# Clearing a slot table in eight paced parts, first gram matrices in one product, spare products from later on, and a new order of work

## The chip, the cores and the metric

The kernel runs on one core of one Trainium2 chip. The metric is the device time of one execution in microseconds (us), the median of several runs; lower is better. The core has a matrix engine (PE in the profile; its weight loads are shown as PEld), a vector engine (DVE), a scalar engine (ACT), a general engine (POOL) and a queue engine (SP) that issues most transfers. All of them run side by side and wait for each other by semaphores.

## The reference

Three stages follow each other. The attention is a delta rule over 768 steps for 2 x 8 heads of 48 columns; its output, 1536 rows of 384 columns, goes through a dense layer pair with a softmax-weighted hidden layer and a norm; the rows that come out are sent to one of 8 experts by the largest logit.

```python
for t in range(S):                                   # S = 768, per batch and head
    y[t] = q[t] @ state
    state = state + beta[t] * outer(k_n[t], v[t] - k_n[t] @ state)
h = x @ w_in                                         # 1536 x 384 by 384 x 1024
e = exp(h - max(h)); sm = e / sum(e)
solu = h * sm
ln = (solu - mean) / sqrt(var + 1e-6) * g_ln
x2 = ln @ w_out                                      # 1024 x 384
expert = argmax(x2 @ w_gate)                         # 8 experts, a capacity each
out = gate * (relu(slots @ w1[expert]) @ w2[expert]) # slots: rows of an expert in order of arrival
```

## The kernel before

The attention is done in 24 chunks of 32 steps, in three groups of eight chunks. For a group, gram matrices `G` (line 510) of k with k and of k with q are made on PE, masked on DVE or on ACT and POOL into `A` and `M`, `A` is transposed into `L` on DVE (586), the triangular system in `L` is solved there by some thirty small operations in two lines (595, 598), and transposed back into `Tt` and `Tn` (606, 608). Four pairs of products `Z` (628, 643) join the halves. Then the chunks go one after the other, since each needs the state that the one before it left: `X` (710) on PE, `R` (715) on DVE, two products (723), `ub` on ACT and DVE (731, 689), `dS` (738) on PE, the new state `S` on DVE (683), and `X` again (752). Four copies on ACT (673) take the chunk's output to `xt`; a chunk is then done, which the code calls the event `s1`. Norms of k (464 to 475) come ahead of a group.

The dense layers run beside that, a tile of 128 rows at a time: 18 products into `h` (905), a maximum, an exponential and a product on DVE and ACT (915, 919, 923), transposes `lp` (944), and 24 products into `xb` (954). Until the last chunk there is one buffer for `h`. Every finished tile's rows are scattered by an indirect transfer on POOL (1112) to their places in a table of slots, `xs`, in the chip's main memory. The table's rows must be cleared before that. After the last tile the experts follow (1389 and 1334 for most of them), from rows that are fetched from `xs`.

The order on PE, DVE, ACT and POOL is not the scheduler's: the build runs a planner (`Flow`), in which each chain of work is a generator that yields the engine it needs and a time, and waits for events; at each step the planner takes the chain of best rank, and the instructions are written out in that order. The ranks come from the table `PR`, so that one number moves work all over the first 340 us. Where the plan leaves PE idle long enough, `fill` writes a spare product (1241) that nobody reads. SP's queue takes its transfers in the order in which the planner came to them.

The clearing is the chain `clear` (line 430): one transfer of zeros from a tile `z` to the whole table (439), after which the event `clear` lets the chain `places` begin, which works out where the rows go.

Of the kernel before, what the change touches and what calls it, by code (L numbers as in the profile page):

```python
# [21 lines left out]
GC = 8  # L22
# [12 lines left out]
GATE, TOK, XW = DM, DM + 1, DM + 2  # L35
# [6 lines left out]
TURN = [b * TPB + s for s in range(TPB) for b in range(B)]  # L42
FIRST = [min(128, CAPS[0] - k) for k in range(0, CAPS[0], 128)]
LATE = 3
LAG = 1
WAIT = 0
LAG0 = 2
FILLER = 2
# [1 line left out]
EVA = (0, 1, 1)  # L50
HB = 0
HC = C // 2
PR = {'m0': 1.68, 'x0': 4.63, 'g1': 9.02, 'g2': 3.68, 'lg': 6.61, 'l1': 1.43, 'l2': 3.47, 'wi': 2.29, 'wo': 5.01, 'wog': 1.18, 'n1': 1.36, 'n2': 4.33, 'p1': 4.79, 'p2': 8.87, 'v': 8.16, 'y': 3.1, 'rows': 2.82, 'sx': 3.04, 'xt': 2.51, 'lt': 4.05, 'ft': 2.27}
PASSES = ((0, 0), (0, 1), (1, 0))
PE, DVE, ACT, POOL, DMA = range(5)
DENSE = 0
# [51 lines left out]
class Flow:  # L108
# [8 lines left out]
    def __init__(self, pace, cap, until):  # L117
        self.req = {e: [] for e in self.LAT}
        self.free = {e: 0.0 for e in self.LAT}
        self.pending = deque()  # L120
        self.cur = None
        self.rate, self.cap, self.fill = pace * self.COLS / self.TICK, cap, None
        self.level = self.at = 0.0
        self.floor, self.until = 1500, until if FILLER else 0
        self.cols = {}
        self.banks, self.fill_bank = {}, "h"
        self.mode, self.pool = DENSE, 0.0
        self.n = self.live = 0
# [69 lines left out]
    def run(self):  # L198
        while True:
# [3 lines left out]
            if not c:  # L203
                assert not self.live, "chains that wait for each other"
                return
            if self.fill:
                t = self.free[PE]
                n = min((x[0][0] for x in c if x[1] == PE), default=t + 9)
                if n - t < self.FILL[0] + (0.23 if self.warm(t) else 0.44):
                    t = n  # L210
                t = max(t, self._clear(self.fill_bank or "", PE))
                if any(self.fill_bank in r[5].split() and r[1] < t + 0.25 for o in self.req if o != PE
                       for r in self.req[o] if r[5] is not None):
                    t = n + 9
                if t < min(x[0][0] for x in c):
                    c = [((t, None), PE)]
# [63 lines left out]
def build(tc, I, out, cap, dbg=None, pace=1.15, room=100):  # L280
# [10 lines left out]
    with ctx:  # L291
# [24 lines left out]
        def us(nbytes):  # L316
            return nbytes / 220e3
# [113 lines left out]
        def clear():  # L431

            yield event("wo", FT - 1)
            yield DMA, us(NS * XW * 4)
            yield WT_
            z = wd.tile([128, XW], F32, name="z", tag="wT")
            nc.gpsimd.memset(z, 0.0)
            nc.gpsimd.memset(z[:, TOK:], FAR)
            nc.sync.dma_start(out=xs.rearrange("(n p) w -> p n w", p=128),
                              in_=z.unsqueeze(1).to_broadcast([128, NS // 128, XW]))  # L440
            WT_.release()
            event("clear").set()

# [109 lines left out]
        def prep(g):  # L555
# [9 lines left out]
                mw = one.tile([128, NI, C], F32, name="mw")  # L565
                fl.spawn(mask_w(g, mw), prio)
            AM[g] = (A, M, mw)
            if g:
                fl.spawn(grams(g, range(0, GC, 2), ((0, 1),)), PR['g1'] if g == 1 else PR['g2'])
            else:  # L570
                for k in range(2):
                    fl.spawn(grams(g, (0, 4), ((k,),)), prio + PR['m0'] * k)
                    fl.spawn(grams(g, (2, 6), ((k,),)), prio + PR['m0'] * k)
            if g:
                yield event("w", g)
            for c in range(0, GC, 2):
# [460 lines left out]
        def places():  # L1037
# [3 lines left out]
            for i, j in enumerate(TURN):  # L1041
                yield event("OH", j)
                pos, g, dist, ov = (posn[:, k, j:j + 1] for k in range(4))
                if i < NTILE - 1:
                    yield DVE, _dv(E)
                    nc.vector.tensor_tensor(out=CO[:, i + 1], in0=CO[:, i], in1=OH[:, j], op=ALU.add)
                    fl.loose()
# [512 lines left out]
```

## Time and profile before

| | us |
|---|---|
| median of 3 runs (495.34 to 499.2) | 498.14 |
| the profiled execution's own time | 496.29 |
| its span from the first to the last instruction | 494.4 |
| PE busy | 445.8 (90%) |
| DVE busy | 286.7 (58%) |
| ACT busy | 240.7 (49%) |
| POOL busy | 168.5 (34%) |

The span falls into four stretches: until 41.7 us the first group is prepared, until 292.8 us the chunks run with the dense layers beside them, until 343.8 us the rest of the dense layers, and then the experts. The profiled execution took 1.9 us more than its span. Its time lies within those of the three runs.

### The profile page before, as it was taken

Reading aid. Unit: us, or ns where it says so; the run is one execution under the profiler, and the core shown is the slowest. Engines: PE = TensorE matmul, PEld = TensorE weight load, DVE = VectorE, ACT = ScalarE, POOL = GpSimd, SP = SyncE. Lnnn points to the kernel's source line nnn. Section 1 sums busy time; section 2 is a strip of 40 time slices with the busy share of each in tenths; the row PEclk is TensorE's granted clock in tenths of the full one; section 3 lists DMA queues with packets and bytes.
Section 4 is the critical chain, followed back from the end, with each engine's and each line's share of the span. In section 5 each row is a group of like instructions: output and inputs, shape, how many; then the busy total and the mean of one; then the engine's idle time right before and its main releaser. Section 6 shows DMA issues by size and latency. Waiting matters only on the chain.

```text
span 494.4 us, 16769 instructions
## 1 busy us (share of the span) xinstructions
PE 445.8 (90%) x7220; PEld 380.1 (77%) x7220; DVE 286.7 (58%) x839; ACT 240.7 (49%) x556; POOL 168.5 (34%) x177
## 2 busy tenths in 40 slices
PE   7696697789949989799999999999999999999993
PEld 3446586667837777687777778898999999999993
DVE  5576486678713354787544466775465554654640
ACT  3012266756513333545445366762574775665620
POOL 1301454111200033211110023343486386669721
PEclk9696568959965989899999999999999999999998
DMA  8371335214390000000000014410887456586100
GB/s 300 84 306 57 103 116 184 66 38 177 125 339 8 3 21 21 3 16 18 20 3 3 4 38 141 153 57 19 294 320 249 158 188 211 189 293 210 75 24 27
DMA packets 16948, 57.58 MB, mean 116 GB/s; under 512 B 2328, under 2 KB 8326, under 8 KB 16098
## 3 DMA queue, kind: packets, MB, share of 16 engines
q1 hardware_dynamic: 15042, 51.70, 30.5%
q0 software_dynamic: 1824, 4.73, 2.6%
q8 instruction: 58, 0.95, 0.8%
q14 instruction: 24, 0.20, 0.1%
HBM read 45.96 MB, written 11.13 MB: 115 GB/s over the span
## 4 chain that ended last, share of the span: by engine, by line
PE 66%; DVE 9%; issue 9%; DMA 7%; ACT 5%; POOL 2%; SPq 1%; POOLq 0%; DVEq 0%; ACTq 0%
PE xb L954 11%; PE h L905 10%; PE u L1389 8%; PE o L1334 7%; PE X L710 5%; PE dS L738 4%; DMA out<-y,ti 3%; PE h L1241 3%; PE G L510 2%; PE X L752 2%; PE lp L944 2%; PE Z L643 2%; PE o L1427 2%; PE Z L628 1%; DMA xd<-xs 1%
## 5 line engine op out<-in xcount | busy, mean ns | idle before, releaser
L1206 POOL TENSOR_TENSOR wh<-wr,wh 128x512 fp32r<-128x512 f32 x64 | 81.7, 1304 | 24.6 <-ACT wh L1204 21.0
L905 PE MATMUL h<-wi,xT 128*128 128x512 f32 x216 | 66.0, 429 | 0.0
L954 PE MATMUL xb<-wo,lT 128*128 128x392 f32 x288 | 66.0, 369 | 0.0
L1334 PE MATMUL o<-wh,hT 128*128 128x384 f32 (+1 forms) x336 | 63.4, 341 | 0.3 <-DVE hT L1393 0.3
L1389 PE MATMUL u<-xdT,wh 128*128 128x240 f32 (+1 forms) x504 | 60.3, 278 | 1.0 <-DVE hT L1393 1.0
L1389 PEld LDWEIGHTS u<-xdT,wh 128*128 128x128 f32 x504 | 59.0, 189 | 1.6 <-DVE hT L1393 1.5
L1334 PEld LDWEIGHTS o<-wh,hT 128*128 128x128 f32 (+1 forms) x336 | 57.4, 182 | 0.8 <-DVE hT L1393 0.6
L954 PEld LDWEIGHTS xb<-wo,lT 128*128 128x128 f32 x288 | 52.4, 197 | 2.5 <-issue 0.5
L673 ACT COPY xt<-X 32x192 f32<-32x192 f32 x96 | 29.7, 310 | 37.4 <-PE X L752 36.2
L905 PEld LDWEIGHTS h<-wi,xT 128*128 128x128 f32 x216 | 39.8, 198 | 8.1 <-issue 0.7
L1204 ACT CAST wh<-wr 128x512 fp32r<-128x512 f32 x67 | 40.8, 616 | 5.8 <-DMA wr<-w 5.8
L1393 DVE SCALAR_TENSOR_TENSOR hT<-u,hT 128x240 fp32r<-128x240 f32 (+2 forms) x64 | 25.0, 409 | 28.8 <-ACT hT L1392 28.1
L710 PE MATMUL X<-S,kqT 48*64 48x48 f32 x768 | 32.2, 239 | 4.8 <-issue 2.8
L710 PEld LDWEIGHTS X<-S,kqT 48*64 48x64 f32 x768 | 28.7, 153 | 9.6 <-issue 5.2
L1392 ACT ACTIVATE hT<-u 128x240 fp32r<-128x240 f32 (+2 forms) x64 | 23.9, 376 | 22.3 <-PE u L1389 20.1
L731 ACT ACTIVATE ub<-X,slot 128x96 f32<-128x96 f32 x48 | 13.7, 335 | 34.6 <-PE X L723 34.2
L1346 POOL DMA_INDIRECT out<-y,ti x17 | 16.5, 972 | 37.6 <-ACT y L1322 11.0
L1112 POOL DMA_INDIRECT xs<-xo,posi x12 | 12.7, 1057 | 48.4 <-ACT lT L983 15.8
L715 DVE TENSOR_TENSOR R<-X,vt 128x384 f32<-128x384 f32 x24 | 13.3, 555 | 27.3 <-PE X L710 26.2
L738 PE MATMUL dS<-ub,kn 64*48 64x96 f32 x368 | 24.5, 284 | 3.5 <-ACT ub L731 3.4
L1241 PEld LDWEIGHTS <-ones 128*32 128x32 bf16 x168 | 13.6, 102 | 18.0 <-issue 6.3
L510 PE MATMUL G<-kqT 48*32 48x32 f32 (+1 forms) x1024 | 21.0, 233 | 6.9 <-issue 6.3
(197 smaller groups left out, 787.3 us busy)
## 6 DMA issues: line engine op xcount, KB each, us to landing
wr<-w SPq DMA_DIRECT2D x32, 768.0 KB, 5.1
kqT<-kqT SPq DMA_DIRECT2D x6, 1024.0 KB, 6.2
xs<-z SPq DMA_DIRECT2D x1, 5597.0 KB
w<-w_in SPq DMA_DIRECT2D x6, 512.0 KB, 4.1
w<-w_out SPq DMA_DIRECT2D x8, 384.0 KB, 3.2
kn<-kN SPq DMA_DIRECT2D x3, 768.0 KB, 8.5
vt<-vN SPq DMA_DIRECT2D x3, 768.0 KB, 11.2
xd<-xs SPq DMA_DIRECT2D x10, 193.0 KB, 4.9
```

Source lines behind the costliest of these rows:

```text
L510: nc.tensor.matmul(G[32 * r:32 * r + 32, c2 * 4 + Q], lhsT=kq[:, r1], rhs=x, start=True, stop=True)
L673: nc.scalar.copy(out=xt[s][32 * j:32 * j + 32, :, 96 * r:96 * r + 96] .rearrange("p b (l d) -> p b l d", l=2), in_=ps_[c % 2][p:p + 32, :, ...
L710: nc.tensor.matmul(ps[64 * o:64 * o + 64, q, r1], lhsT=T[p, c % HG, q // 2, r1, q % 2], rhs=S_[p, q, r1], start=(q == 0 and r1 == 0), stop ...
L738: nc.tensor.matmul(dS[64 * o:64 * o + D, q], lhsT=kn_t[g][64 * o:64 * o + 64, cc, q], rhs=ub[64 * o:64 * o + 64, q], start=False, stop=Tru ...
L905: nc.tensor.matmul(h[:, FH * n:FH * n + FH], lhsT=xT[a][:, k], rhs=wi[w][:, k, FH * n:FH * n + FH], start=(m == 0), stop=(m == 3 * KT - 1))
L954: nc.tensor.matmul(x2, lhsT=lT[t // 4][a][:, t % 4], rhs=wo[w][:, t], start=(t == 0 and i == 0), stop=(t == FT - 1 and i == 2))
L1204: nc.scalar.copy(out=hl[0][:, cs], in_=r[:, cs])
L1206: (nc.vector if k == 1 else nc.gpsimd).tensor_tensor(out=hl[1][:, cs], in0=r[:, cs], in1=hl[0][:, cs].bitcast(F32), op=ALU.subtract)
L1241: nc.tensor.matmul(spare[0], lhsT=ones[:, 0:32], rhs=ones[:, 0:spare[0].shape[1]], start=spare[0].shape[1] > 120, stop=True, skip_group_ch ...
L1334: nc.tensor.matmul(o, lhsT=hT[t][a][:, s:s + n], rhs=w[k][:, t % 4], start=(t == 0 and i == 0), stop=(t == FT - 1 and i == 2))
L1389: nc.tensor.matmul(u, lhsT=w[c][:, k, f0:f0 + 128], rhs=xT[a][:, k], start=(i == 0 and k == 0), stop=(i == 2 and k == KT - 1))
L1393: nc.vector.scalar_tensor_tensor(out=hh[1], in0=u, scalar=0.0, in1=hh[0].bitcast(F32), op0=ALU.max, op1=ALU.subtract)
```

## The change

The clearing is cut into eight transfers, of 3 or 4 times 128 rows of the table each. Each is preceded by a transfer of a single number from the output of chunk 9, 10, ... 16 to the first of the part's rows, so that the part is issued only once that chunk is done. The event `clear` comes after the fifth part, the new event `clear all` after the eighth; the third tile's placing waits for that one. The first group's gram matrices are made as those of the other groups are, k with k and k with q in one product of 64 columns, where there were two of 32. Spare products are written only from 28 us of the plan on; the limit that the planner was given before was not used. Several ranks in `PR` are new, and with them the order on every engine. `m0` was the rank step of the first group's grams, which is no longer read. No DVE, ACT or POOL instruction is added or removed.

```diff
-PR = {'m0': 1.68, 'x0': 4.63, 'g1': 9.02, 'g2': 3.68, 'lg': 6.61, 'l1': 1.43, 'l2': 3.47, 'wi': 2.29, 'wo': 5.01, 'wog': 1.18, 'n1': 1.36, 'n2': 4.33, 'p1': 4.79, 'p2': 8.87, 'v': 8.16, 'y': 3.1, 'rows': 2.82, 'sx': 3.04, 'xt': 2.51, 'lt': 4.05, 'ft': 2.27}
+PR = {'m0': 4.99, 'x0': 4.63, 'g1': 4.24, 'g2': 3.44, 'lg': 6.61, 'l1': 1.43, 'l2': 3.47, 'wi': 2.29, 'wo': 5.01, 'wog': 1.18, 'n1': 1.36, 'n2': 4.17, 'p1': 4.79, 'p2': 8.87, 'v': 8.16, 'y': 5.65, 'rows': 2.82, 'sx': 3.04, 'xt': 6.94, 'lt': 3.58, 'ft': 2.8}
...
-            if self.fill:
+            if self.fill and self.free[PE] >= self.until:
...
             yield event("wo", FT - 1)
-            yield DMA, us(NS * XW * 4)
             yield WT_
+            yield POOL, 0.5
             z = wd.tile([128, XW], F32, name="z", tag="wT")
             nc.gpsimd.memset(z, 0.0)
             nc.gpsimd.memset(z[:, TOK:], FAR)
-            nc.sync.dma_start(out=xs.rearrange("(n p) w -> p n w", p=128),
-                              in_=z.unsqueeze(1).to_broadcast([128, NS // 128, XW]))
+
+
+            n = NS // 128
+            at = [NCOL * i // CLEAR for i in range(CLEAR)] + [NCOL + (n - NCOL) * i // 3 for i in range(4)]
+            for i, (a, b) in enumerate(zip(at, at[1:])):
+                c = GC + 1 + i
+                yield event("s1", c)
+                yield from gate(xt[c // 4][32 * (c % 4):32 * (c % 4) + 1, 0, 0:1], xs[128 * a:128 * a + 1, 0:1])
+                yield DMA, us(128 * (b - a) * XW * 4)
+                nc.sync.dma_start(out=xs[128 * a:128 * b].rearrange("(n p) w -> p n w", p=128),
+                                  in_=z.unsqueeze(1).to_broadcast([128, b - a, XW]))
+                if b == NCOL:
+                    event("clear").set()
             WT_.release()
-            event("clear").set()
+            event("clear all").set()
...
-            if g:
-                fl.spawn(grams(g, range(0, GC, 2), ((0, 1),)), PR['g1'] if g == 1 else PR['g2'])
-            else:
-                for k in range(2):
-                    fl.spawn(grams(g, (0, 4), ((k,),)), prio + PR['m0'] * k)
-                    fl.spawn(grams(g, (2, 6), ((k,),)), prio + PR['m0'] * k)
+            fl.spawn(grams(g, range(0, GC, 2), ((0, 1),)), (prio, PR['g1'], PR['g2'])[g])
...
+                if i == 2:
+                    yield event("clear all")
```

SP's queue after the second group's weights and the third group's loads, before (`xs` is the table of slots, `z` the tile of zeros, `wr` the first expert's weights):

```order
L383 DMA kqT<-kqT 128x2048
L392 DMA vt<-vN 128x1536
L439 DMA xs<-z 128x29x386
L1183 DMA wr<-w 128x1536 x2
L1135 DMA x_4860<-xs 128x384
```

The same place after the change, up to the third part:

```order
L384 DMA kqT<-kqT 128x2048
L393 DMA vt<-vN 128x1536
L402 DMA xs<-xt 1x1
L449 DMA xs<-z 128x3x386
L402 DMA xs<-xt 1x1
L449 DMA xs<-z 128x3x386
L402 DMA xs<-xt 1x1
L449 DMA xs<-z 128x4x386
```

One transfer of 29 times 128 rows became eight pairs, and they stand between the last load of the attention and the first load of the experts, so nothing else in the queue waits behind them until the first expert's weights.

DVE in the last steps of the first group's solve, before (`sq` are squares of the second group's k, which its load must bring first; `nn` their sums):

```order
L598 TENSOR_TENSOR L<-L,tmp 128x2x4x11
L464 TENSOR_REDUCE nn<-sq 128x8
L595 TENSOR_TENSOR tmp<-L 128x72
L598 TENSOR_TENSOR L<-L,tmp 128x2x3x12
L595 TENSOR_TENSOR tmp<-L 128x52
L464 TENSOR_REDUCE nn<-sq 128x8
L598 TENSOR_TENSOR L<-L,tmp 128x2x2x13
L595 TENSOR_TENSOR tmp<-L 128x28
L598 TENSOR_TENSOR L<-L,tmp 128x2x14
L464 TENSOR_REDUCE nn<-sq 128x8
L600 MEMSET L 128x32
L606 STREAM_TRANSPOSE Tt<-L 128x32x32
```

The same stretch after:

```order
L605 TENSOR_TENSOR L<-L,tmp 128x2x4x11
L602 TENSOR_TENSOR tmp<-L 128x72
L605 TENSOR_TENSOR L<-L,tmp 128x2x3x12
L602 TENSOR_TENSOR tmp<-L 128x52
L605 TENSOR_TENSOR L<-L,tmp 128x2x2x13
L476 TENSOR_REDUCE nn<-sq 128x8
L602 TENSOR_TENSOR tmp<-L 128x28
L605 TENSOR_TENSOR L<-L,tmp 128x2x14
L607 MEMSET L 128x32
L476 TENSOR_REDUCE nn<-sq 128x8
L613 STREAM_TRANSPOSE Tt<-L 128x32x32
```

The first sum over the second group's squares stands four steps of the solve later, the second one six.

PE between the first product of chunk 8 and that of chunk 9, before (`xb` are the dense layers' products):

```order
L710 MATMUL X_136<-S,kqT 64x48 x16
L944 MATMUL lp<-idn,p 128x128 x4
L643 MATMUL Z<-z,Tn 32x16 x16
L723 MATMUL X_136<-R,Tt 32x48 x8
L723 MATMUL dS<-R,Tt 32x48 x8
L944 MATMUL lp<-idn,p 128x128 x4
L954 MATMUL xb<-wo_142,lT_2244 128x392
L954 MATMUL xb<-wo_143,lT_2244 128x392
L954 MATMUL xb<-wo_142,lT_2245 128x392
L954 MATMUL xb<-wo_142,lT_2244 128x392
L738 MATMUL dS<-ub,kn 48x96 x8
```

After:

```order
L717 MATMUL X_136<-S,kqT 64x48 x16
L840 MATMUL tp<-idn,wu 128x128 x3
L635 MATMUL Z<-Tt,A 32x16 x16
L730 MATMUL X_136<-R,Tt 32x48 x8
L730 MATMUL dS<-R,Tt 32x48 x8
L635 MATMUL Z<-Tt,A 32x16 x32
L745 MATMUL dS<-ub,kn 48x96 x8
L759 MATMUL X_136<-ub,M 32x48 x16
L635 MATMUL Z<-Tt,A 32x16 x16
```

The dense layers' products left the place, and small products of the second group's joins came to it. In counts over the whole order: ahead of chunk 8 there are 36 products into `h` where there were 54, and 18 into `xb` where there were 24; behind the first product of the last chunk there are 72 into `h` where there were 54, 138 into `xb` where there were 107, and 40 transposes `lp` where there were 32. Of spare products of 512 columns there is 1 where there were 90; of 120 columns into `xb` there are 75 where there were 13.

## Rows read from the trace of the kernel before

**Rows 1.** Page, part 2: busy tenths of PE and its clock in 40 slices.

```profile
PE   7696697789949989799999999999999999999993
PEclk9696568959965989899999999999999999999998
```

**Rows 2.** Stretches: length, then busy us (count) by engine, clock, DMA share, GB/s.

```profile
139.62:160.10 20.48, 17.02 (x260) 13.84 (x260) 5.80 (x16) 5.66 (x13) 1.31 (x3) 0.50 0.43 145
...
292.81:343.77 50.96, 49.53 (x421) 44.30 (x421) 33.16 (x138) 28.15 (x61) 17.39 (x21) 1.00 0.26 89
343.77:494.40 150.63, 141.35 (x1039) 138.99 (x1038) 76.88 (x174) 83.06 (x183) 90.04 (x75) 0.99 0.54 184
```

**Rows 3.** Timeline of the first group: start, length, engine, line, idle before.

```profile
13.35 0.76 DVE L528 TENSOR_TENSOR A<-G,mw 128x256 f32<-128x256 f32 x2 [2.02 <-POOL mw L551]
...
19.05 2.07 DVE L586 STREAM_TRANSPOSE L<-A 128x1024 f32<-128x1024 f32 x1
...
29.37 0.52 ACT L462 ACTIVATE sq<-kn 128x384 f32<-128x384 f32 x1 [4.69 <-DMA kn<-kN]
29.92 0.55 DVE L464 TENSOR_REDUCE nn<-sq 128x8 f32<-128x384 f32 x1 [2.31 <-ACT sq L462]
...
32.86 1.95 DVE L606 STREAM_TRANSPOSE Tt<-L 128x1024 f32<-128x1024 f32 x1
...
36.60 1.19 PEld L628 LDWEIGHTS Z<-Tt,A 32*32 32x32 f32 x128 [0.42 <-DVE M L528]
```

**Rows 4.** Chain that ended last, first 45 us: start, length, what.

```profile
18.30 1.93 PE G L510 x128
20.23 1.52 issue
...
38.51 1.95 issue
...
41.76 1.88 PE X L710 x32
```

**Rows 5.** Timeline around the clearing.

```profile
130.81 0.41 SPq L439 DMA_DIRECT2D xs<-z  x1
...
140.66 0.60 PE L643 MATMUL Z<-z,Tn 32*32 32x16 f32 x27 [4.29 <-issue]
...
147.82 1.01 PE L944 MATMUL lp<-idn,p 128*128 128x128 f32 x4 [2.42 <-issue]
```

**Rows 6.** Page, parts 3 and 6: instruction queue (packets, MB, share) and the clearing.

```profile
q8 instruction: 58, 0.95, 0.8%
...
xs<-z SPq DMA_DIRECT2D x1, 5597.0 KB
```

**Rows 7.** Chain that ended last, chunks 8 to 13.

```profile
162.37 1.06 PE X L710 x32
...
168.50 1.06 PE X L710 x32
...
177.38 1.33 issue
...
183.35 1.01 PE G L510 x32
```

**Rows 8.** Two us inside the clearing, and two beside the `G` at 183.35.

```profile
136.00:138.00 2.00, 0.37 (x7) 0.14 (x5) 0.56 (x1) 0.55 (x2) 0.30 (x1) 1.00 1.06 360
182.00:184.00 2.00, 2.00 (x78) 1.70 (x74) 1.20 (x5) 0.57 (x2) 1.97 (x4) 0.50 0.29 107
```

**Rows 9.** Chain that ended last, from the last chunk on.

```profile
292.81 1.13 PE X L710 x32
...
300.61 2.09 PE h L905 x9
...
303.46 4.31 PE xb L954 x24
...
331.70 1.10 PE x0p L1241 x19
```

More of the change, by code (lines that the diff above doesn't have):

```diff
@@ L44 @@
 LATE = 3
+CLEAR = 5
 LAG = 1
@@ L123, in __init__ @@
         self.level = self.at = 0.0
-        self.floor, self.until = 1500, until if FILLER else 0
+        self.floor, self.until = 1500, until
         self.cols = {}
```

## The prediction

> **What bounds the kernel now.** I read the slices of the page first, then the stretches, then the chain that ended last with the timeline beside it. The slices show PE busy at nine tenths or more in the last half, at full clock, and the holes in the first: slices where PE is at four to seven tenths, and its clock at five to nine [rows 1]. The experts take 150.63 us, 141.35 of it busy on PE, and the change leaves them alone; the rest of the dense layers ahead of them, behind the last chunk's first product, is 50.96 us with 49.53 busy [rows 2]. Both are bound by PE's own work. So what the change can win or lose lies ahead of 292.81, where that product starts [rows 9]: the time in which PE waits there, and the time in which it works at half clock. Two places concern the change.
>
> The first group is a chain with nothing beside it. The first masked write of `A` is at 13.35, the solve on DVE begins with the transposing at 19.05, and PE starts the first join at 36.60, after a late write of `M` [rows 3]. On the way DVE stands 2.31 us at a sum over the second group's squares, since the load of that k has landed only at 29.37 [rows 3].
>
> The clearing is one transfer of 5597 KB [rows 6], issued at 130.81 and moved at some 360 GB/s with the transfer engines full [rows 8]. PE stands 4.29 us until 140.66 and 2.42 us until 147.82 with no engine named that it waits for [rows 5], and works at half clock from 139.62 to 160.10 [rows 2]. Such stops have a pattern: between the one that ended at 18.30 and the next, 1.52 us long, PE ran exactly 128 loads and 128 products [rows 4], and the instruction queue moved 58 packets of 0.95 MB in all [rows 6], 16 KB each. I read the stops as PE waiting for its next piece of 256 instructions. Away from the clearing they take 1.3 to 2.0 us [rows 4, 7]; the longest stands inside it.
>
> **First group: 2.0 us less (0 to 3).** No spare product comes ahead of the grams now, so I price them at half clock, as at 183.35: 32 rows, which are 16 products of 64 columns, take 1.01 us [rows 7, 8], a pair of chunks 2.0. Two pairs can be done before the mask at 13.35. Each of the other two needs a buffer, free once `A` and `M` of an earlier pair are written, twice 0.4: the third runs from 14.2 to 16.2, the fourth to 18.3, and its `A` and `M` end at 19.1, where the transposing starts now at 19.05. The stop that ended at 18.30 goes with the smaller number of instructions, and half clock takes its place: no gain up to here. In the solve the first sum stands four steps later, and two sums stand ahead of the transposing instead of three. The load still lands at 29.4, the sum ends at 30.4, then two steps of 0.2, the second sum, and the transposing starts at 31.5 instead of 32.86. The join doesn't wait for `M` any more and starts at 33.5 instead of 36.60. Of these 3 us one is lost, since DVE has the remaining sums and a weight's splitting, some 3.5 us, ahead of the first joined write, and the stop of 1.95 us ahead of the second joins [rows 4] hangs on 256 instructions and stays. The first chunk's `X`, at 41.76 [rows 4], comes at 39.7.
>
> **Clearing: 6.4 us less (2 more to 14.2 less).** Now it costs 4.29 + 2.42 = 6.7 us of stops, and 17.02 us of PE's work at half clock [rows 2, 5]. `X` takes 1.88 us at half clock [rows 4] and 1.06 at full [rows 7], so 17.02 x (1 - 0.56) = 7.5 us would go at full clock; together 14.2. Two things come back. A part is 579 or 772 KB and fills the engines for 2.0 us at 360 GB/s, while chunks follow each other in 6.1 us (168.50 - 162.37) [rows 7]; so SP's queue keeps pace, and nothing stands behind a part in it. But each part may hold up a piece of instructions, by 0 to 2.0 us. PE takes a piece in some 4 us there, so about half the parts meet one, and I take half the bound: 8 x 0.5 x 1.0 = 4.0. And chunks 8 to 10 have the second group's joins beside them now, small products that use up pieces fast, in place of `xb`: a stop like the 1.33 us at 177.38 is to be expected, and shortly behind that one the clock stood at half as well [rows 7, 8]. So I let half of the 7.5 come back, 3.8. That leaves 14.2 - 4.0 - 3.8 = 6.4.
>
> The rows' placing starts later, after chunk 13, and for the third tile after chunk 16. Finished rows wait in six buffers, and the order has two placings ahead of chunk 17, so I cost this at nothing; if those buffers were full, `xb` would stop.
>
> [...]
>
> **New order: 1 us less (9 more to 5 less).** Ahead of chunk 8, PE has 18 products into `h` less, at 2.09 / 9 = 0.23 us, and 6 into `xb`, at 4.31 / 24 = 0.18 [rows 9]: 5.2 us that must be done later. Behind the last chunk's first product it has 18 and 31 more, 4.2 + 5.6, with the transposes some 11 us. PE's sum doesn't change, so this wins or loses only as far as the chunks come earlier by more or less than 11 us: the last chunk has to start at 282 to break even. I expect about that. The second group's solve stands beside chunks 4 to 6, where it stood beside 5 to 7, with its joins up to 141 as the last thing ahead of chunk 8 [rows 5]; but its steps stand close together on DVE there, and will hold up the chunks 4 to 6 themselves.
>
> **Spare products: 0.5 us more (0 to 3.6).** 62 more into `xb`, at 1.10 / 19 = 0.058 us [rows 9], are 3.6 us. They stand where the plan has PE idle, and cost only as far as the trace is later than the plan. The 89 large ones that go stood in waits for loads and for the solve, and give back nothing.
>
> **Sum.** 2.0 + 6.4 + 1.0 - 0.5 = 8.9 us less. On the profiled execution, 494.4 and 1.9 around it, that is 487.4; on the median of 498.14 it is 489.2. I take 488.3, midway.
>
> **Rivals.** *The clearing's cost is spread and not removed.* The same 5.6 MB go through the same engines, in the stretch where PE uses up pieces fastest. If nearly every part meets one, 8 x 2.0 = 16 us of stops stand against 14.2, the term is nothing, and 498.14 - 2.0 - 1.0 + 0.5 = 495.6 is left. For it: the 4.29 us stood in the middle of the clearing, not at its end. Against: gaps of 4 us between parts of 2 us leave a piece room. [...]
>
> *The chunks don't come earlier, and the dense work behind them does harm.* The place is behind chunk 23: 11 us more stand there. Chunks took 6.1 us each with PE's holes filled [rows 7], and emptying the holes doesn't shorten a chain that goes through DVE and ACT. If the last chunk starts at 291, earlier by the first group's 2 us alone, 9 of the 11 us come on top: 498.14 - 2.0 + 11 = 507. It is slower than before once the last chunk starts behind 282, and by over 1% behind 287. Against: the clearing's stops and half clock lie ahead of that chunk too, and a share of them is certain to go.
>
> *More than forecast.* If no clock is lost, no piece is late and the solve is hidden, it is 498.14 - 2.0 - 14.2 - 4.5 + 0.5 = 478.
>
> **How the numbers follow.** A measurement of this kernel tells a change from none at about 1%: outside 493.2 to 503.1. The forecast, with half of the clearing's cost gone or more, has 0.54 (480 to 493.2); more than that 0.06; the clearing spread, or small terms all round, 0.27, within 1%; the dense work behind the chunks 0.13, of which 0.10 is over 503.1 and 0.03 within. Faster 0.60, same 0.30, slower 0.10. The range of 477 to 499 holds the forecast, the full gain and the spread clearing, and leaves out 0.03 below and some 0.15 above.
>
> **What the profile after would show.** The first `X` near 39.7, and DVE's wait for the squares still there but shorter. No stop of 4 us on PE between chunks 7 and 9, and chunk 8 well before 141. Eight parts on SP's queue, 6 us or more apart, with stops under 2 us on PE beside half of them. The last chunk at 270 to 280, and some 62 us from there to the experts. I am wrong if PE stops once per part, if the half clock returns for longer than 10 us around chunks 8 to 10, or if the last chunk starts behind 287.

## The result, and the profile after

The changed kernel took 477.17 us (median of 4 runs, 476.32 to 477.91), the kernel before 496.74 beside it (4 runs, 494.39 to 499.2). The ratio is 0.9605, its 95% interval 0.9548 to 0.9662. So 19.6 us were won, where 9 were forecast. Medians are over all executions, here and below; the ratios leave out those of over 1.5% above the fastest of the same kernel. The profiled execution took 477.91, its span is 476.1: 18.3 less than before. Of these 5.0 lie ahead of the first `X` and 13.8 between it and the experts; the experts took 0.5 more.

The page's slices of PE and its clock, after [rows 1]:

```profile
PE   2328978989999999999999999999999999999983
PEclk9999995988659999999999999999999999999998
```

PE's holes between the first group and the experts are nearly gone. The clock's first slices mislead: the chip's record of it has no entry ahead of 61.96 there, and the page shows full speed, but 128 rows of `G` took 3.68 us and an `X` 1.88. Where the granted clock was 0.50 before, 32 such rows took 1.01 us [rows 7, 8] and an `X` 1.88 [rows 4] (0.50 from 41.7 to 44.0); where it was 1.00, 32 rows took 0.58 us, at 145.39 after, and an `X` 1.06 [rows 7] (1.00 from 160.1 to 165.0 before). So I estimate that much of that stretch ran at half clock: 3.68 is nearer to four times 1.01 than to four times 0.58.

The stretches after: chunks 0 to 6, chunk 7 with the second joins, chunks 8 to 11, chunks 12 to 22, from the last chunk to the experts, the experts [rows 2].

```profile
36.78:98.94 62.16, 53.22 (x1363) 43.61 (x1363) 55.73 (x122) 38.05 (x94) 25.36 (x23) 0.92 0.36 117
98.94:120.14 21.20, 19.32 (x429) 15.66 (x428) 13.51 (x35) 12.37 (x27) 5.81 (x7) 0.84 0.34 127
120.14:151.70 31.56, 30.53 (x802) 25.42 (x801) 7.76 (x18) 8.76 (x28) 5.08 (x7) 0.68 0.01 4
151.70:263.40 111.70, 109.92 (x2319) 85.31 (x2318) 69.61 (x239) 54.73 (x137) 17.64 (x28) 1.00 0.18 65
263.40:324.93 61.53, 60.51 (x488) 54.32 (x487) 40.41 (x171) 35.71 (x74) 19.15 (x25) 1.00 0.22 77
324.93:476.10 151.17, 141.01 (x1040) 139.21 (x1038) 78.61 (x175) 83.40 (x183) 90.05 (x75) 0.98 0.54 184
```

Chunk 8 starts at 120.1 (141.2 before), the last chunk at 263.4 (292.8), and from there to the experts it takes 61.5 us (50.96 before [rows 2]). So 24.4 us were won in the chunks behind the first `X`, and 10.6 given back behind the last. Half clock did not go: the mean is 0.68 over chunks 8 to 11, and in the chain that ended last `X` takes 1.88 us at both ends of it:

```profile
120.20 1.88 PE X L717 x32
...
135.76 1.88 PE X L717 x32
```

The first group's timeline after [rows 3, 4]:

```profile
18.32 1.97 DVE L593 STREAM_TRANSPOSE L<-A 128x1024 f32<-128x1024 f32 x1
...
27.06 0.52 ACT L474 ACTIVATE sq<-kn 128x384 f32<-128x384 f32 x1 [3.45 <-DMA kn<-kN]
...
28.86 0.55 DVE L476 TENSOR_REDUCE nn<-sq 128x8 f32<-128x384 f32 x1 [0.21 <-ACT sq L474]
29.33 1.91 DVE L613 STREAM_TRANSPOSE Tt<-L 128x1024 f32<-128x1024 f32 x1
...
36.06 0.71 PE L650 MATMUL Z<-z,Tn 32*32 32x16 f32 x35 [1.11 <-issue]
36.71 1.95 PE L717 MATMUL X<-S,kqT 48*64 48x48 f32 x32
```

DVE's wait for the squares is gone but for 0.21 us, since they start at 27.06 and not at 29.37. The first three clearing parts on SP's queue:

```profile
154.74 0.42 SPq L449 DMA_DIRECT2D xs<-z  x1
...
158.16 0.38 SPq L449 DMA_DIRECT2D xs<-z  x1
...
161.62 0.38 SPq L449 DMA_DIRECT2D xs<-z  x1
```

They begin at 154.74, behind the second group's joins, and no stop of PE over 0.7 us stands behind 131 us until the experts. The pacing alone didn't put them there: the number from chunk 9 was sent at 134.78, and the first part then waited 19.0 us for POOL, which came to setting `z` only at 154.1. The second and third follow 3.4 us apart. What PE waited for from the first `X` to the experts is the view that tells most. The costliest rows before (us in total, times, the longest; "issue" is a wait with no engine named):

```profile
PE Z L643 <- issue: 7.5, 3, 4.3
PE X L723 <- DVE R L715: 3.9, 4, 1.9
PE dS L738 <- ACT ub L731: 3.4, 3, 1.6
PE X L710 <- issue: 2.8, 1, 2.8
PE G L510 <- issue: 2.5, 2, 1.3
PE lp L944 <- issue: 2.4, 1, 2.4
```

and after:

```profile
PE X L730 <- DVE R L722: 3.2, 4, 1.5
PE G L522 <- issue: 2.6, 1, 2.6
PE dS L745 <- ACT ub L738: 2.2, 2, 1.1
PE gp L850 <- ACT wu L791: 1.1, 1, 1.1
PE X L730 <- issue: 1.0, 1, 1.0
PE Z L635 <- issue: 0.7, 1, 0.7
```

All rows of that view sum up by what was waited for: before 16.7 us of issue, 8.4 of DVE, 3.6 of ACT; after 4.3, 6.0 and 4.1. PE was busy for about as long (272.4 and 273.6), with 3.7 us more of spare products among that. So 12.4 of the 14.3 us by which the waits fell are stops with no engine named, of which the prediction had counted only the two beside the clearing, 6.7.

Those stops have their place in common. Each of them stands where PE has used up another 256 instructions, its sequencer's counted in: at the 193rd, the 449th and so on, in all 16 profiles of this study. Mostly the time since the last such place plus the stop is 2.9 to 4.4 us: 1.93 + 1.52 before at 20.2, 1.31 + 1.95 at 38.5, 1.56 + 1.33 at 177.4, 2.35 + 1.11 after at 34.95, 2.43 + 1.03 at 129.5. Pieces that PE worked on for over 3.6 us show none but for three. At five, these three among them, the sum is larger: before 4.57 + 2.83 at 53.0, 5.65 + 1.34 at 78.8 and 2.72 + 4.29 and 4.75 + 2.42 beside the clearing, 7.0 to 7.4 each, and after 3.17 + 2.55 at 69.95. There the transfer engines were busy to 0.85 and more. One wait with no engine named is of another kind: 1.78 us until 13.96 after, elsewhere in the count; there `G` starts 0.1 us behind the write of an `M`, which frees a buffer. Two us each before and after, just ahead of the stops at 78.8 and 69.95 (clock, DMA share and GB/s are the last three columns), to be held against [rows 8]:

```profile
76.00:78.00 2.00, 2.00 (x94) 1.71 (x92) 1.90 (x7) 1.39 (x6) 1.19 (x2) 1.00 1.06 422
```

```profile
68.00:70.00 2.00, 1.95 (x82) 1.64 (x71) 1.44 (x5) 1.77 (x6) 0.32 (x1) 1.00 0.85 356
```

So in these two traces a piece that ended in a stop lasted some 3.6 us, 2.9 at the least, and up to 7.4 beside large transfers, the clearing being one of several.

The stops go with the packets of the instruction queue, 16 KB each [rows 6]. The 16 profiles have 112 such stops of over 0.5 us, 12 of them before and 4 after; each ends 1.2 to 1.6 us behind the end of a packet, one 0.9. Before, the packets that ended at 139.07, 146.33 and 177.34 are followed by PE's starts at 140.66, 147.82 and 178.71. At the ordinary stops of the two traces the packet starts 0.6 to 1.9 us behind the beginning of the piece and takes 0.9 to 1.9; at the five long ones it starts 3.4 to 5.1 us behind, and takes 0.9 to 1.0. So at these five, beside large transfers, the packet started later and did not take longer. Two packets went while the clearing was still moving at some 350 GB/s, at 138.19 and 145.36, so neither waited for its end.

At all 11 ordinary stops of the two traces the packet started while PE was still working on the piece, and at two of the five long ones, 4.7 us into pieces of 5.65 and 4.75. The shortest, of 2.9 us at 178.71, is made up of 0.55 until the packet started, 0.97 for the packet and 1.36 behind it.

For the later experiments, planned without the packets, I made a sum from the pairs above: 3.6 us, an estimate, less the time of each piece up to the experts where that is shorter, from a kernel's own trace with its stops taken out. It gives 13.5 us before and 3.8 to 4.5 after, by how a place is found among products that overlap; the stops themselves, those ahead of the first `X` included, were 22.4 and 5.4.

### The profile page after: what moved, and what is told of

Same layout as the page of the kernel before. It is cut to its first block, busy times and chain, and to the rows that moved or that the text cites. A ratio compares the mean times of both kernels' runs of the same rounds, so it can differ in the third digit from the quotient of the medians.

```text
span 476.1 us, 16248 instructions
## 1 busy us (share of the span) xinstructions
PE 425.9 (89%) x6941; PEld 374.2 (79%) x6941; DVE 291.8 (61%) x839; ACT 240.8 (51%) x556; POOL 168.8 (35%) x177
## 4 chain that ended last, share of the span: by engine, by line
PE 72%; DVE 13%; issue 5%; ACT 4%; DMA 3%; POOL 1%; SPq 0%; POOLq 0%; DVEq 0%; ACTq 0%
PE h L912 12%; PE u L1398 12%; PE xb L961 11%; PE o L1343 10%; PE X L717 5%; PE dS L745 3%; PE G L522 3%; PE lp L951 2%; PE X L759 2%; PE o L1436 2%; DMA out<-y,ti 2%; PE Z L650 2%; PE X L730 1%; DMA kqT<-kqT 1%; DVE wu L798 1%
## 5 line engine op out<-in xcount | busy, mean ns | idle before, releaser
L961 PE MATMUL xb<-wo,lT 128*128 128x392 f32 x288 | 63.5, 360 | 0.0
L961 PEld LDWEIGHTS xb<-wo,lT 128*128 128x128 f32 x288 | 50.1, 191 | 2.3
L680 ACT COPY xt<-X 32x192 f32<-32x192 f32 x96 | 29.7, 310 | 25.7 <-PE X L759 24.4
L522 PE MATMUL G<-kqT 48*32 48x64 f32 x768 | 19.8, 269 | 13.1 <-DMA kqT<-kqT 8.5
L522 PEld LDWEIGHTS G<-kqT 48*32 48x32 f32 x768 | 16.5, 140 | 15.6 <-DMA kqT<-kqT 8.5
L1209 DVE CAST wh<-wp 128x512 fp32r<-128x512 f32 x29 | 20.0, 691 | 9.8 <-ACT wp L1208 8.5
```

The costliest lines, as they stand in the source:

```text
L522: nc.tensor.matmul(G[32 * r:32 * r + 32, c2 * 4 + Q], lhsT=kq[:, r1], rhs=x, start=True, stop=True)
L680: nc.scalar.copy(out=xt[s][32 * j:32 * j + 32, :, 96 * r:96 * r + 96] .rearrange("p b (l d) -> p b l d", l=2), in_=ps_[c % 2][p:p + 32, :, ...
L961: nc.tensor.matmul(x2, lhsT=lT[t // 4][a][:, t % 4], rhs=wo[w][:, t], start=(t == 0 and i == 0), stop=(t == FT - 1 and i == 2))
```

## Experiments

The theories at the start: the clearing's place beside the joins cost what was won (A), or the new order did, by itself (B). Later ones: the pieces of 256 instructions, and what brought the first `X` forward. Times of the kernel before beside each run were medians of 495.09 to 497.03; each ratio is to that kernel. Unless said otherwise, the order on PE, DVE, ACT and POOL is that of the kernel from which each starts.

**One transfer instead of eight, in the changed kernel, at the first part's place.**

```diff
-                nc.sync.dma_start(out=xs[128 * a:128 * b]..., in_=z...[128, b - a, XW])
+                if i == 0:
+                    nc.sync.dma_start(out=xs..., in_=z...[128, n, XW])
```

> The changed kernel with the clearing in one transfer again, issued where its first part was; the order on PE, DVE, ACT and POOL is that of the changed kernel, instruction by instruction. If the cutting won the larger part (theory A: stops and half clock of one large transfer), this loses 6 to 14 us against the changed kernel's 477.2, so 483 to 491, with a stop of some 4 us on PE beside the transfer. If the new order won it, by filling PE's idle time and moving the clearing away from the second group's joins (theory B), it loses under 3 us: 477 to 480.

480.11 us (478.38 to 482.37), ratio 0.9697 (0.9595 to 0.9798). That is 2.9 more than with parts by the medians and 4.6 by the two ratios, whose intervals overlap. The transfer ran from 156 us on, and no stop of PE over 0.7 us stands beside it. So the cutting is worth some 3 to 5 us, less than theory A's 6 to 14, and nothing isn't excluded.

**A transfer of 5.6 MB that nobody reads, behind chunk 7 of the changed kernel, beside the second joins.**

```diff
+            yield event("s1", GC - 1)
+            nc.sync.dma_start(out=x2.rearrange("(n p) w -> p n w", p=128),
+                              in_=src.unsqueeze(1).to_broadcast([128, NS // 128, XW]))
```

> The changed kernel with a transfer more that nobody reads, as large as the whole clearing, issued once chunk 7 is done, beside the second group's joins, where the kernel before had its clearing; the order on the other engines is unchanged. Theory A: a stop of 4 us and more on PE in the joins, half clock behind it, 6 to 14 us more than 477.2: 483 to 491. Theory B: under 3 us more: 477 to 480.

485.92 us (484.43 to 487.31), 8.75 more. PE's timeline in the joins:

```profile
124.69 0.71 PE L658 MATMUL Z<-z,Tn 32*32 32x16 f32 x34 [5.79 <-issue]
```

This large transfer beside the joins did cost that much, in the new order too.

**The kernel before with its clearing in four parts, behind chunks 8 to 11.**

```diff
+            for i in range(4):
+                a, b, c = n * i // 4, n * (i + 1) // 4, GC + i
+                yield event("s1", c)
+                nc.sync.dma_start(out=xs[128 * a:128 * a + 1, 0:1], in_=xt[c // 4][...])
+                nc.sync.dma_start(out=xs[128 * a:128 * b]..., in_=zz[0]...)
```

> The kernel before, its order on PE, DVE, ACT and POOL unchanged, with the clearing in four parts, each issued after chunk 8, 9, 10 and 11, where it was one transfer ahead of chunk 8. Theory A: the stops of 4.29 and 2.42 us and the half clock from 139.6 to 160.1 go, 6 to 14 us less than 496.7, so 483 to 491. Theory B (the stops and the half clock come with the joins' small products, with or without the transfer): under 3 us less, 494 to 498.

494.28 us (488.63 to 499.45), ratio 0.9965 (0.9919 to 1.0011): no gain. The stop beside the second joins fell to 0.73 us, but the last part was issued at 163.72 and met the third group's joins:

```profile
136.62 0.42 PE L655 MATMUL Z<-z,Tn 32*32 32x16 f32 x27 [0.73 <-issue]
...
171.69 0.41 PE L655 MATMUL Z<-z,Tn 32*32 32x16 f32 x17 [5.47 <-issue]
```

**The kernel before with its clearing in one transfer, but behind chunk 8.** The same lines with one part and `c = GC`.

> The kernel before, in its own order, with the clearing still in one transfer, but behind the result of chunk 8, so that it moves from some 145 to 161 us: behind the second group's joins and ahead of the third's. Theory A (what the clearing costs is its lying beside the joins, where pieces of instructions are used up fast): chunk 7 to 8 takes 27 us instead of 31.1 and chunk 8 to 9 7 to 8 instead of 12.7, the third group's joins have no stop over 2 us, and the time is 8 to 12 us less, 484 to 488. Rival B (a transfer of this size costs the same beside any part of the chunks): within 3 us of 496.

490.07 us (487.51 to 491.97), ratio 0.9889 (0.9793 to 0.9986): 6.3 less by the medians, 5.5 by the ratio, between the two theories. In the profile the clearing is issued at 148.19, chunk 7 to 8 takes 27.7 us and 8 to 9 8.9, but a stop of 2.45 us came in the third joins. The place is worth some 6, less than expected, in a wide interval.

**The new table of priorities alone, on the kernel before** (a new order everywhere).

```diff
-PR = {'m0': 1.68, ... 'g1': 9.02, ... 'y': 3.1, ... 'xt': 2.51, ...}
+PR = {'m0': 4.99, ... 'g1': 4.24, ... 'y': 5.65, ... 'xt': 6.94, ...}
```

> The kernel before with the new table of ranks alone; the plan makes its own order of it, which is neither that of before nor of after. Theory B: most of the 19.6 us, so 478 to 486. Theory A: the first group's part of it and little more, 489 to 495.

491.33 us (487.54 to 494.61), ratio 0.9900 (0.9855 to 0.9946): 5.0 less by the ratio, in theory A's range and far from B's. The single clearing transfer moved to 158.21 by the order alone, so its move is within these 5.0. Issue is 9.7 us of PE's waits, 7.0 less than before, and PE's idle time 8.8 less; 4.8 us of that went to more spare products. The first `X` stayed at 42.0.

**The changed kernel with the old table** (the same lines the other way round; a new order everywhere).

> The changed kernel with the old table of priorities; clearing in parts, single gram products and later spare products are kept. Theory A (the table is what fills PE's holes among the chunks, over 10 us of the 13.8): 486 to 492. Rival B (most of the 13.8 comes from the other three parts, the clearing away from the joins above all, and the table gives back what it wins in the tail): 476 to 481.

488.43 us (487.5 to 496.27): 11.3 more. First `X` at 36.3, chunk 8 even earlier than after (114.0), the last chunk at 274.9. Issue is 8.4 us, DVE 9.8.

**The changed kernel with the first group's grams in two products** (a new order everywhere).

```diff
-            fl.spawn(grams(g, range(0, GC, 2), ((0, 1),)), (prio, PR['g1'], PR['g2'])[g])
+            if g:
+                fl.spawn(grams(g, range(0, GC, 2), ((0, 1),)), PR['g1'] if g == 1 else PR['g2'])
+            else:
+                for k in range(2):
+                    fl.spawn(grams(g, (0, 4), ((k,),)), prio + PR['m0'] * k)
+                    fl.spawn(grams(g, (2, 6), ((k,),)), prio + PR['m0'] * k)
```

> The changed kernel with the first group's gram matrices in two products again, k's and q's apart; the planner places everything anew. Theory A (the single products are worth 3 to 5 us at the first X, and what is won there is passed on to the end): first X at 39.5 to 42, time 480 to 483. Rival B (later waits absorb it): first X at 39.5 to 42, and the time within 1.5 us of 477. Rival C (the single products are not what brought the first X forward): first X at 36 to 38.

484.46 us (484.04 to 486.88): 7.3 more, but the first `X` at 36.6, as rival C had it, and `L` at 17.0. Issue is 8.4 us, half of it one stop behind the first chunk:

```profile
45.20 0.23 PE L640 MATMUL Z<-Tt,A 32*32 32x16 f32 x1 [3.81 <-issue]
```

**No spare products in the changed kernel.**

```diff
-            nc.tensor.matmul(spare[0], lhsT=ones[:, 0:32], rhs=ones[:, 0:spare[0].shape[1]],
-                             start=spare[0].shape[1] > 120, stop=True, skip_group_check=True)
+            pass
```

> The changed kernel in its own order, with all 145 spare products left out, and nothing put in their place. Theory A (spare products stand in PE's waits and cost only the half microsecond that I gave them): the time within 1 us of 477.2, and the granted clock stays at full where they stood. Rival B (they are PE's work as any other, 10.05 us of it on PE ahead of the experts): 3 to 8 us less, 469 to 474. Rival C (they hold the clock up): without them half clock comes back behind chunk 13 or ahead of the experts, and the time rises by 2 to 8 us, to 479 to 485.

478.06 us (475.45 to 481.19), 0.9 more, within the runs' spread. PE's idle time between first `X` and experts went from 14.7 to 19.7 us as 10.0 us of spare products left, but its other work took 4.3 us longer, so the stretch was only 0.6 us shorter. Theory A's second half didn't hold: from 211.0 to 217.8 us the granted clock was half, where it is 1.00 in the changed kernel. There spare products had stood at 209.3 to 209.7 and 212.7; without them PE was busy for 2.01 of the 3 us ahead. The mean clock from the first `X` to the experts is 0.92, against 0.93. That is theory C's sign, in the profile of the longest of the five executions; in the median its time is not seen.

**Two more transfers behind the second group's k, in the changed kernel.**

```diff
             yield from load_kq(3)
+            nc.sync.dma_start(out=x2, in_=I["vN"][:, GC:2 * GC])
+            nc.sync.dma_start(out=x3[:, 0:2], in_=I["kqT"][:, 0:2])
```

> The changed kernel in its own order, with two more transfers, 768 and 512 KB from inputs to a scratch tensor in memory, on SP's queue directly behind the loads of the second group's k and of kqT, where the kernel before has a weight and v on the way at the same time. Nothing reads them. Theory A (the first group won 5.0 us and not 2.0, because the second group's k landed earlier, its load having less beside it): the first squares on ACT start later than 27.06, at 28.5 to 29.5, DVE waits 1 to 2.3 us for them at a sum as it did before, the first X comes at 38 to 39 instead of 36.8, and the time rises by 1 to 2 us, to 478 to 479.5. Rival B (the single products and the missing mask of M alone did it, and the sums' place in the order): the first X stays within 0.5 us of 36.8 and the time at 477.

481.38 us (480.45 to 481.96), 4.2 more, but by neither theory: the squares start at 27.04, as without them. The stops in the first joins grew instead:

```profile
36.93 0.71 PE L654 MATMUL Z<-z,Tn 32*32 32x16 f32 x35 [1.85 <-issue]
...
43.95 0.23 PE L639 MATMUL Z<-Tt,A 32*32 32x16 f32 x2 [3.47 <-issue]
```

They were 1.11 and 0.72, and the first `X` came at 37.57 and not at 36.71. These transfers, queued behind the load of k, did not delay it: from its issue to the squares' start it took 7.1 us with them and 7.3 without. It took 7.0 to 7.3 us in 14 of the 16 profiles of this study, and 8.6 and 8.7 in two of the kernel before and its order, in which four other runs had 7.2 to 7.3.

**Instructions taken away: 40 spare products less in the first solve of the kernel before.**

```diff
+            calls[0] += 1
+            if 33 < calls[0] <= 73:
+                return
             nc.tensor.matmul(spare[0], lhsT=ones[:, 0:32], ...)
```

> The kernel before, in its own order, with 40 of the 56 spare products left out that PE makes between 22 and 36.6 us while it waits for the first solve. Nothing else is changed; what is left out are 80 of PE's instructions, so all later pieces of 256 instructions begin 80 instructions further on in the work. Theory A (PE stops wherever 256 instructions are used up in less than some 3.6 us, and the changed order wins by having fewer such places): with the trace of before, 3.6 us less the time that each piece took, summed over the pieces up to the experts, gives 13.5 us with the pieces as they lie and 8.7 with them 80 instructions on, so 4.8 us less, or more where the clearing stretches a stop; 488 to 493, and the stops of 4.29 and 2.31 us beside the clearing change their size and place. Rival B (stops come from the transfers and from the waits of the work itself): within 1.5 us of 496.

490.79 us (486.76 to 495.05), ratio 0.9891 (0.9793 to 0.9990): 5.6 less by the medians, 5.4 by the ratio. Issue fell from 16.7 to 9.7 us behind the first `X` in the profile, that of the longest of the four executions, where the first `X` stands at 43.9. The long stop beside the clearing stayed, at 4.42; the second, of 2.42, is gone.

**Instructions added: 72 products of 8 columns in place of 24 of 512 there.**

```diff
+            if 33 < calls[0] <= 57:
+                for _ in range(3):
+                    nc.tensor.matmul(spare[0][:, 0:8], lhsT=ones[:, 0:32], rhs=ones[:, 0:8], ...)
+                return
```

> The kernel before, in its own order, with 24 of the spare products that PE makes while it waits for the first solve replaced by 72 of 8 columns, which take about the same time. PE has 96 instructions more, and later pieces of 256 begin 96 instructions earlier in the work. Theory A (the pieces): the sum of 3.6 us less each piece's time goes from 13.5 to 16.9; 498 to 501, against 490.8 with 40 products less. Rival B (it is the spare products' time that costs): no change, within 1.5 us of 496.

496.52 us (494.19 to 503.19) beside 495.09, ratio 1.0068 (1.0027 to 1.0108): slower by 0.7%, or 3.4 us; by the medians it is 1.4. The sign is that of theory A, but longer stops are not what the profile shows: from the first joined products on, issue is 17.4 us against 18.7 in the kernel before, and of that 12.7 against 16.7 lie behind the first `X`, which comes at 45.11 here. The other waits are 13.9, against 12.0.

**32 products of 8 columns at the start of the changed kernel.**

```diff
+        for _ in range(32):
+            nc.tensor.matmul(spare[0][:, 0:8], lhsT=ones[:, 0:32], rhs=ones[:, 0:8], ...)
```

> The changed kernel in its own order, with 32 more spare products of 8 columns at its very start, where PE waits for kqT until 8.5 us. They are 64 instructions, so each later piece of 256 begins 64 instructions earlier in the work. Theory A (the pieces): the sum of 3.6 us less each piece's time rises from 3.8 to 7.0 us; 479.5 to 482, with two or three stops of over 1 us more. Rival B (stops don't hang on where the pieces begin): within 0.7 us of 477.2.

480.79 us (479.93 to 482.21), 3.6 more. They themselves took 1.02 us, in a wait. The size is what theory A gave, but the profile doesn't show its way: there the first `X` stands at 36.5, a stop of 2.67 us came at 41.3, the one of 2.55 went, and issue is 4.0 us in all. Waits for DVE and ACT rose from 10.1 to 15.2.

**The first 88 spare products left out of the kernel before.**

```diff
+            if 0 < calls[0] <= 88:
+                return
```

> The kernel before, in its own order, without the first 88 spare products, which stand ahead of, among and behind the first group's gram matrices. The gram matrices are in two products each, as before. Theory A (the spare products, and the pieces of instructions that they use up, are what held the first group back, and not the second product): the transposing on DVE starts at 16.8 to 17.8 instead of 19.05, the first X comes at 37 to 39 instead of 41.7, and what is won is lost again in part behind it, since the pieces then lie where the sum of theory A of the run with 40 spare products less gives 16.8 us instead of 13.5; 492 to 496. Rival B (the second product held it back): the transposing at 18.5 to 19.5, and the first X at 40 to 42.

492.45 us (489.93 to 496.49), ratio 0.9986 (0.9929 to 1.0043). `L` stands at 16.88, `Tt` at 29.37, as early as after; but two stops of 1.38 and 1.83 us stand ahead of the first `X`, at 40.53:

```profile
36.64 1.51 PE L643 MATMUL Z<-z,Tn 32*32 32x16 f32 x97 [1.38 <-issue]
...
40.37 0.23 PE L628 MATMUL Z<-Tt,A 32*32 32x16 f32 x1 [1.83 <-issue]
40.53 1.94 PE L710 MATMUL X<-S,kqT 48*64 48x48 f32 x32
```

**77 early spare products put into the changed kernel**, 27 ahead of the grams and 50 behind them.

```diff
+        def early(n):
+            for _ in range(n):
+                nc.tensor.matmul(h_[0][0:32, :512], lhsT=ones[:, 0:32], rhs=ones[:, 0:512], ...)
...
             for c in range(0, GC, 2):
                 yield event("A", g, c)
+            if g == 0:
+                early(50)
...
+        early(27)
         fl.free[DVE] = 2.5
```

> The changed kernel in its own order, with 27 spare products of 512 columns put ahead of the first group's gram matrices and 50 behind them, while PE waits for the first solve, about as the kernel before has them. The gram matrices stay single products. Theory A (the later spare products brought the first X forward, by the time and the pieces of instructions that the early ones take): the transposing on DVE starts at 19 to 20.5 instead of 18.3, the first X comes at 38.5 to 41, and the time is 2 to 4 us more, 479 to 481. Rival B (the single products did it, and spare products in waits cost nothing): first X at 36.5 to 37.5, and the time within 1 us of 477.

483.26 us (480.0 to 488.17), but `L` at 18.07 and the first `X` at 36.41: rival B in the group, and not in the time. Behind the first `X` three stops with no engine named, of 1.0 to 2.2 us, and a wait of 1.7 for `R` stand until 54 us.

## Why the prediction was right in sign and wrong in size

**First group, 2.0 forecast, 5.0 measured.** Mis-sized at three steps. "The load still lands at 29.4": it landed at 27.06, since its issue moved with the group's `A` from 20.77 to 19.79, and since it took 7.3 us and not 8.6; that is 2.2 us of `Tt`. "no gain up to here": 0.7. "The stop ... stays": it fell from 1.95 to 1.11. The 5.0 is one profile against one: the same first group came to its first `X` at 42.60 and 44.51 in the two variants that only move the clearing, and the changed one at 36.45 and 36.85 in the two whose only edit is one large transfer. Which edit did it is only half settled. Two gram products without early spare products and with the new table give the same first `X` (36.6) as single ones with early spare products (36.4); both together, in the kernel before, hold the group back. The old order with neither single products nor early spare ones has `Tt` as early as after, but two stops hold its first `X` until 40.5.

**Clearing, 6.4 forecast.** The size came near, by luck: two errors cancel. The half clock that I let come back in part did so in full, so the 3.7 us of clock were not won: 31.56 us at a mean of 0.68 are some 20 at half, as long as before [rows 2], which the prediction named as a sign that it would be wrong. And the stops that I let come back, 4.0 us in all, came nowhere, though the first parts were 3.4 us apart and not 6. What went were the two stops, 6.7 us. Moved away from the joins in the old order, the transfer was worth some 6, so the cause is the place more than the eight parts, which are worth 3 to 5 at most; parts that still meet joins won nothing.

**Spare products, 0.5 forecast.** Without them the time was 0.9 more, within the spread: no cost is seen. Whether they keep the clock up, as that run's profile suggests, stays open.

**New order, 1 forecast: the step that failed.** "the last chunk has to start at 282 to break even. I expect about that." It started at 263.4. The tail's price was right (62 forecast, 61.5 measured), so what is left for the order is some 7 us net where 1 was forecast: 13.8 between the first `X` and the experts, less the 6.7 of the two stops. That is a subtraction between two traces and no run's result: the table alone, with the clearing's move in it, gave 5.0. What the step left out is that PE's stops don't only lie at the clearing. I had read the pieces of 256 instructions in the trace, and then priced two of the nine stops behind the first `X` and left the other seven, 10.0 us, out of the sum; 5.7 of them went. Where small products of the joins and grams stood in a row, a piece was used up in 1.3 to 3.5 us, and PE stood until 1.2 to 1.6 us behind a packet's end, once 0.9. Which edit shortened the seven is not settled. The table alone brought issue from 16.7 to 9.7 us, but 6.7 of these 7.0 are the two stops beside the clearing, which it moved; the others went from 10.0 to 9.7. Issue is 8.4 in the changed kernel with the old table, 8.4 with two gram products, and 4.3 only with all edits together. That the new order wins by mixing small products with chunks and dense ones is likely from the orders, and not shown; that other pieces happen to begin in better places would do the same.

**How far that is shown.** That PE's waits fell by 14.3 us, 12.4 of it such stops, is read from the two traces, and that a stop ends 0.9 to 1.6 us behind a packet of instructions in all sixteen. Moving the pieces without touching the order moved the time three times with the sign that the sum gave (5.6 for 4.8; 3.6 for 3.2; 1.4 or 3.4 for 3.4). The first and the last have intervals that leave out no change, if narrowly (0.9793 to 0.9990, 1.0027 to 1.0108); the 3.6 is a difference between medians that were not taken beside each other, and the intervals of the two ratios overlap. Counted in these runs' own traces, the sum is about 10.0, 15.5 and 5.9 us, where 8.7, 16.9 and 7.0 were expected: the sign again, with smaller steps. That it goes through longer or shorter stops is seen in one of these three profiles only; in the other two the waits for DVE and ACT grew, from 10.1 to 15.2 us and from 12.0 to 13.9. That a small delay early on changes which engine is late next is my estimate from these, and one profiled execution does not separate that. The edits don't add up either: taking one back cost 11.3 (table), 7.3 (grams) and 2.9 us (parts), together more than the 19.6, since each gives the planner another order.

**The rivals.** "More than forecast" named 478 us, which is the time that came, by other terms: it had the clock back in full, and 4.5 us for the order that it worked out nowhere. "Clearing spread" and "the chunks don't come earlier" fell with the traces. None of the variants was faster than the changed kernel by its median.

## What to carry to other kernels

Before pricing a new order, count PE's instructions: at every 256th, where all 112 stops stood here, look at how long the last 256 took and whether a stop stands there, for all of them and not only for the longest; a stop that ends just behind a packet of the instruction queue, 1.2 to 1.6 us here, is of this kind. Many of the stops lay in runs of small products (10.6 of the 16.7 us before stood ahead of `Z` and `G`), so large transfers want to lie away from such runs (one beside them cost 8.75 us); cutting the transfer up won nothing where a part still met them (ratio 0.9965, 0.9919 to 1.0011). Mixing small products with large ones is worth a try, though no run here shows its gain by itself. When a term comes out right, add up its parts: here two wrong ones cancelled. And one profiled execution's duration is one draw: the load that a term hung on took 8.6 us there and 7.2 mostly.

## What was not expected of the hardware

Where PE stopped went with the number of instructions ahead: each of the 112 stops stands where another 256 were used up. In the two traces a piece that ended in a stop lasted 2.9 to 4.4 us, and 5.7 to 7.4 with transfers of 300 to 420 GB/s beside it, where the packet ahead of the stop's end started 3.4 to 5.1 us into the piece and not 0.6 to 1.9. With 80 instructions less in a wait the kernel was 1.1% faster, with 96 more 0.7% slower, with the same work behind them. Two transfers of 1.3 MB in all, queued behind a load, did not delay it (7.1 us from its issue to the first squares, 7.3 without them), but the two stops of PE in the first joins were 1.85 and 3.47 us with them and 1.11 and 0.72 without.
